# Windowed attention with a split-precision FFN on one core: where the values and scores of the next units stand in TensorE's queue

## The chip, the core and the metric

The kernel runs on one NeuronCore of a Trainium2 chip. The number that counts is the device time of one execution in microseconds. Before the change it is 905.27 us, the median of three runs (904.88 to 905.30). Below, PE is TensorE, PEld its weight loads, DVE is VectorE, ACT is ScalarE, POOL is GpSimd and SP is SyncE, whose queue issues most of the transfers.

## The reference

For 8 batches, 8 heads, 576 positions and head size 64, every position attends to itself and to the 63 positions before it. The result, 4608 tokens of 512 numbers, goes through an FFN with a leaky ReLU of slope 0.01:

```
scores = scale * np.matmul(q, k.transpose(0, 1, 3, 2))
mask = (rel >= 0) & (rel < window)              # window = 64
attn = softmax(np.where(mask, scores, -1e9))
x = np.matmul(attn, v)                          # laid out as 4608 x 512
h = x @ w_in                                    # 512 x 2048
g = np.maximum(0.01 * h, h)
out = g @ w_out                                 # 2048 x 512
```

## The kernel before

**The two halves.** Attention works on units of 64 query positions of one batch, all 8 heads at once; there are 72, and a "visit" handles two. The FFN works on chunks of 512 tokens (nine of them, `c`), which is eight units or four visits of attention. Every chunk runs through 16 column tiles (`f`) of 128 columns of the hidden layer.

**One step of the FFN.** A step is one pair of (c, f). `mm1` (L457) makes the column tile: 12 matmuls of 128x128 weights on 512 tokens, because each operand is the sum of a high and a low part (`x`, `wi`) and three of the four products are taken. The result lands in a PSUM bank named `h`. ACT makes the leaky ReLU `g` from it ("leak", L462) and the rounded high part `gh` (L468), and DVE the low part `gl` (L472). `mm2` (L504) multiplies `gh` and `gl` with `wo`, again 12 matmuls, into four accumulators `acc` that stay open over the 16 steps of a chunk. `mm2` always runs one step behind: a step issues `mm1` of its own tile and then `mm2` of the tile before it. After the sixteenth `mm2` of a chunk, four copies (L530) and four transfers (L531) write the chunk's output.

**One visit of attention.** From the third chunk on (`c` = 2 to 8, 112 steps numbered `n`) a visit is spread over two steps of every four. In the step with `n % 4 == 1`:

- `values_2(u)` (L419): 32 matmuls of 64 columns that multiply the finished probabilities `e` of units u and u+1 with `v`; then SP is told to load the next `v` (L145).
- `scores_2(u+2)` (L234): 64 matmuls of 64x64, the scores of the next two units, into two PSUM banks `s`; then SP is told to load the next `k` and `q` (L141, L137).
- `shield_2(u+2)`: DVE scales and masks both banks into `e` (L380, twice), POOL takes the maximum over the keys (L388, once per half), DVE subtracts the first maximum (L393), ACT takes the first exponential (L394).
- `invert_2(u)`, after `mm2`: two additions and a reciprocal on DVE (L431 to L433) of the sums `n`.

In the step with `n % 4 == 2`: `second_2(u+2)` subtracts and exponentiates the second half (L393, L394), `norm_2(u)` multiplies the values with the reciprocal and writes their high and low part into the `x` of the next chunk (L440, L443, L444), and `sums_2(u+2)` lets POOL add up the exponentials (L406, twice).

**What sets the order.** Every engine works through its own queue strictly in the order in which this code issues instructions; the end of the kernel pins that order with an explicit dependency from each instruction to the one before it on its engine. Semaphores between engines come from the tiles that the instructions share. PSUM banks are handed out in turn: `of_h` alternates between the banks "o" and "h" for `mm1`, and `of_a` between "s" and "t". `scores_2` takes one bank of each kind and `values_2` one of `of_a`. The first two chunks run from other loops (a hand-written order, then a loop over 16 jobs), which already has five visits of its own.

Of the kernel before, what the change touches and what calls it, by code (L numbers as in the profile page):

```python
# [82 lines left out]
def flat(t):  # L83
    return t.rearrange("p a b -> p (a b)") if len(t.shape) == 3 else t
# [3 lines left out]
def band_attention_ffn(ctx: ExitStack, tc: tile.TileContext, qT, kB, vW, w_in, w_out, eye_mask, out):  # L88
# [9 lines left out]
    def bank(tag, name):  # L98
        return ps_e.tile([P, 512], F32, tag=tag, name=name)
# [140 lines left out]
    def mask_of(u):  # L240

        kinds = [v % NQB == 0 for v in (u, u + 1)]
        if any(kinds):
            return away[:, 1:] if kinds[0] else away[:, :2]
        return away[:, :1]
# [115 lines left out]
    def scores_2(u):  # L361
        if u >= NU:
            return
        ps = [bank(next(t), f"s{u}_{j}") for j, t in enumerate((of_a, of_h))]
        quarter_scores(u // 2, ps, False)
        probs[u] = ps
        load_k(u // 2 + 1)
        load_q(u // 2 + 2)

    def shield_2(u):  # L370

        if u >= NU:
            return
        ps = probs.pop(u)
        a = mask_of(u).bitcast(F32)
        n = a.shape[1]
        a = flat(a)[:, None, :].broadcast_to([P, H // n, n * QB])
        for j in range(2):
            e, s = (x.rearrange("a (b c) -> a b c", c=n * QB) for x in (probs_of[:, j], ps[j]))
            nc.vector.scalar_tensor_tensor(e, s, SCALE, a, ALU.mult, ALU.add)  # L380
            if j == 0:
                first_most = most(u, j)
        exps_2(0, first_most)
        probs[u] = most(u, 1)

    def most(u, j):
        mx = wk.tile([P, 512], F32, tag="pT", bufs=1, name=f"mx{u}_{j}")
        nc.gpsimd.partition_all_reduce(mx, probs_of[:, j], P, ReduceOp.max)  # L388
        return mx

    def exps_2(j, mx):
        e = probs_of[:, j]
        nc.vector.tensor_tensor(e, e, mx, ALU.subtract)  # L393
        nc.scalar.activation(e, e, AF.Exp)  # L394

    def second_2(u):

        if u < NU:
            exps_2(1, probs.pop(u))

    def sums_2(u):
        if u >= NU:
            return
        raw = flat(wk.tile([P, 512, 2], U32, tag="raw", bufs=3, name=f"n{u}")).bitcast(F32)
        for j in range(2):
            nc.gpsimd.partition_all_reduce(raw[:, 512 * j : 512 * j + 512], probs_of[:, j], P, ReduceOp.add)  # L406
        probs[u] = raw

    def values_2(u):
        if u >= NU:  # L410
            return
        raw = probs.pop(u)
        v = [v_heads(u // 2, w) for w in range(2)]
        ps = bank(next(of_a), f"o{u}")
        for w in range(2):
            for p in range(NP):
                for j in range(2):
                    c = (2 * p + w) * QB
                    nc.tensor.matmul(  # L419
                        ps[64 * j : 64 * j + 64, c : c + QB], v[w][:, 2 * p + j, :D], probs_of[:, j, c : c + QB],  # L420
                        start=True, stop=True,
                    )
        probs[u, 0] = ps, raw
        load_v(u // 2 + 1)

    def invert_2(u):
        if u >= NU:
            return
        ps, raw = probs[u, 0]
        r, t = raw[:, :512], raw[:, 512:]  # L430
        nc.vector.tensor_scalar_add(r[:64], r[:64], 1e-9)  # L431
        nc.vector.tensor_scalar_add(r[64:], t[64:], 1e-9)
        nc.vector.reciprocal(r, r)  # L433

    def norm_2(u):
        if u >= NU:
            return
        ps, raw = probs.pop((u, 0))
        r, t = raw[:, :512], raw[:, 512:]
        nc.vector.tensor_tensor(t, ps, r, ALU.mult)  # L440
        hi, lo = x_of(u)
        t = t.rearrange("a (b c) -> a b c", b=NP)
        nc.scalar.copy(hi, t)  # L443
        nc.vector.tensor_tensor(lo, t, hi.bitcast(F32), ALU.subtract)  # L444
# [5 lines left out]
    def mm1(c, f, part):  # L450

        xh, xl = xs[c]
        ps = bank(next(of_h) if c or f >= half else "h", f"h{c}_{f}_{part.start}")[:, part]
        wh, wl = wi[f]
        terms = [(a, b, k) for k in range(KT) for a, b in ((wh, xh), (wh, xl), (wl, xh))]
        for n, (a, b, k) in enumerate(terms):
            nc.tensor.matmul(ps, a[:, k, :], b[:, k, part], start=n == 0, stop=n == len(terms) - 1)  # L457
        t = []

        def leak():  # L460
            t.append(wk.tile([P, CH], F32, tag="g", bufs=1, name=f"g{c}_{f}_{part.start}")[:, part])
            nc.scalar.activation(t[0], ps, AF.Prelu, alpha=0.01)  # L462

        def high():
            g[c, f, part.start] = [
                wk.tile([P, CH], F32R, tag=n, name=f"{n}{c}_{f}_{part.start}") for n in ("gh", "gl")
            ]
            nc.scalar.copy(g[c, f, part.start][0][:, part], t[0])  # L468

        def low():  # L470
            hi, lo = (x[:, part] for x in g[c, f, part.start])
            nc.vector.tensor_tensor(lo, t[0], hi.bitcast(F32), ALU.subtract)  # L472

        return leak, high, low
# [13 lines left out]
    def mm2(c, f, part):  # L488


        gh, gl = g.pop((c, f, part.start))
        wh, wl = wo[f]
        for i in range(part.start // P, part.stop // P):
            split = c == 1 or c == 0 and i < 2
            begin = f == 0 or split and f == half
            end = f == FT - 1 or split and f == half - 1
            if begin:
                pool, tag = (ps_o, f"o{i}")
                if c == 1 and f == 0 and i > 1:
                    pool, tag = ps_e, "st"[i - 2]  # L500
                acc[c, i] = pool.tile([P, DM], F32, tag=tag, name=f"acc{c}_{i}_{f}")
            ts = slice(i * P, (i + 1) * P)
            for n, (a, b) in enumerate(((gh, wh), (gh, wl), (gl, wh))):
                nc.tensor.matmul(  # L504
                    acc[c, i], a[:, ts], b, start=begin and n == 0, stop=end and n == 2
                )
            if end:
                due.append(partial(evict, c, i, f, split))
# [24 lines left out]
    def flush():  # L533
        while due:
            due.pop(0)()

    whole, first, second = slice(0, CH), slice(0, CH // 2), slice(CH // 2, CH)
# [33 lines left out]
    def step(name):  # L571
        kind = name.rstrip("0123456789")
        return partial(acts[kind], int(name[len(kind) :]))
# [32 lines left out]
    steps = [(c, f) for c in range(2, NCHUNK) for f in range(FT)]  # L606
    for n, (c, f) in enumerate(steps):
        u = 3 * UPC + n // 4 * 2
        for step in mm1(c, f, whole):
            step()  # L610
        if n % 4 == 1:
            values_2(u)
            scores_2(u + 2)
            shield_2(u + 2)
        if n % 4 == 2:
            second_2(u + 2)
            norm_2(u)
            sums_2(u + 2)
        mm2(*prev)
        flush()  # L620
        if n % 4 == 1:
            invert_2(u)
        prev = (c, f, whole)
# [58 lines left out]
```

## Time and profile before

| | |
|---|---|
| median of the runs | 905.27 us |
| the profiled execution's own time | 906.58 us |
| its span (first to last instruction) | 904.8 us |
| PE busy | 896.4 us (99%) |
| PEld, DVE, POOL, ACT busy | 735.6, 497.2, 321.2, 304.9 us |
| granted TensorE clock | 1.00 |

The profiled execution's time has 1.8 us outside the span and is 1.3 us above the median of the runs. A timeline row gives the start, the duration, the engine, the line of the code, the operation, what it writes and reads, its shape and how many instructions were merged (x12); in brackets stands how long the engine was idle before it and what released it. The ends of matmuls are modelled and overlap the next matmul's start, so PE's pace is read from start to start and not from durations.

### The profile page before, as it was taken

To read this page: it belongs to the slowest core of one execution; us is meant where nothing else is said; L and a number is where in the kernel's file an instruction comes from. 1 tells how busy PE (TensorE), PEld (TensorE's weight loads), DVE (VectorE), ACT (ScalarE), POOL (GpSimd) and SP (SyncE) were. 2 spreads that over 40 slices of the span, in tenths; PEclk is the share of its full clock that TensorE was granted. 3 is DMA by queue.
4 is the path that set the end of the run, shared out by engine and by line. 5 is a ranking of instruction groups with operands and counts; after the bars stand their busy time and mean duration, and the time that the engine had idled before them with its cause. 6 is when DMAs were issued, how large, how long until landed. Compare 5 with 4: busy or idle time off the path is not lost.

```text
span 904.8 us, 16195 instructions
## 1 busy us (share of the span) xinstructions
PE 896.4 (99%) x7021; PEld 735.6 (81%) x7021; DVE 497.2 (55%) x638; ACT 304.9 (34%) x517; POOL 321.2 (36%) x132
## 2 busy tenths in 40 slices
PE   8999999999999999999999999999999999999998
PEld 5887888888888888888888888888888888888886
DVE  6999892388644545555555545444555555531111
ACT  4665654232222232223322222223222332223222
POOL 4422000577433434444444434333434444400000
PEclk9999999999999999999999999999999999999999
DMA  7753741223311011111211121112101221001001
GB/s 286 254 175 116 245 140 70 71 95 119 118 47 47 27 63 53 48 48 47 95 47 49 47 95 47 49 47 85 40 25 40 72 71 36 25 1 47 0 1 47
DMA packets 31895, 68.68 MB, mean 76 GB/s; under 512 B 3024, under 2 KB 3152, under 8 KB 31824
## 3 DMA queue, kind: packets, MB, share of 16 engines
q1 hardware_dynamic: 27360, 51.95, 16.9%
q10 hardware_dynamic: 4464, 15.70, 5.7%
q8 instruction: 55, 0.90, 0.4%
q14 instruction: 16, 0.13, 0.0%
HBM read 56.62 MB, written 11.01 MB: 75 GB/s over the span
## 4 chain that ended last, share of the span: by engine, by line
PE 93%; DVE 4%; issue 1%; DMA 1%; ACT 1%; POOL 0%; ACTq 0%; DVEq 0%
PE acc L504 42%; PE h L457 41%; PE s L234 4%; PE o L419 3%; PE o L323 1%; DMA room<-eye_mask 1%; PE s L268 1%; DVE gl L472 1%; DVE raw L185 1%; DVE w L202 0%; DVE raw L189 0%; DVE raw L197 0%; DVE wi L209 0%; PE s L302 0%; DVE e L293 0%
## 5 line engine op out<-in xcount | busy, mean ns | idle before, releaser
L457 PE MATMUL h<-x,wi 128*128 128x512 f32 (+1 forms) x1440 | 339.1, 384 | 0.1
L457 PEld LDWEIGHTS h<-x,wi 128*128 128x128 f32 x1440 | 265.7, 188 | 54.7 <-DVE x L444 0.4
L504 PE MATMUL acc<-wo,gh 128*128 128x512 f32 x936 | 293.7, 395 | 0.3 <-DVE s L521 0.3
L472 DVE TENSOR_TENSOR gl<-g,gh 128x512 fp32r<-128x512 f32 (+1 forms) x147 | 100.2, 682 | 325.1 <-ACT gh L468 324.9
L388 POOL PARTITION_ALL_REDUCE mx<-e x56 | 108.2, 1933 | 382.1 <-DVE e L380 359.1
L504 PEld LDWEIGHTS acc<-wo,gh 128*128 128x128 f32 x936 | 172.7, 188 | 37.6 <-DVE s L521 0.5
L406 POOL PARTITION_ALL_REDUCE n<-e x56 | 183.2, 3271 | 38.6 <-ACT e L394 38.6
L462 ACT ACTIVATE g<-h 128x512 f32<-128x512 f32 (+1 forms) x147 | 86.6, 589 | 317.0 <-PE h L457 315.8
L504 PE MATMUL acc<-wo,gl 128*128 128x512 f32 x468 | 182.3, 390 | 0.0
L504 PEld LDWEIGHTS acc<-wo,gl 128*128 128x128 f32 x468 | 87.9, 188 | 19.0
L394 ACT ACTIVATE e<-e 128x512 f32<-128x512 f32 x56 | 35.4, 633 | 200.0 <-DVE e L393 200.0
L433 DVE RECIPROCAL n<-n 128x512 f32<-128x512 f32 x28 | 93.9, 3353 | 1.0
L468 ACT CAST gh<-g 128x512 fp32r<-128x512 f32 (+1 forms) x147 | 89.9, 612 | 9.0 <-PE acc L504 4.0
L457 PE MATMUL h<-x,w 128*128 128x512 f32 x324 | 77.8, 389 | 0.0
L444 DVE TENSOR_TENSOR x<-n,x 128x512 fp32r<-128x512 f32 x28 | 61.7, 2202 | 19.2 <-ACT x L443 19.2
L457 PEld LDWEIGHTS h<-x,w 128*128 128x128 f32 x324 | 60.8, 188 | 12.7
L504 PE MATMUL acc<-w,gh 128*128 128x512 f32 x216 | 66.7, 390 | 0.0
L393 DVE TENSOR_TENSOR e<-e,mx 128x512 f32<-128x512 f32 x56 | 38.4, 686 | 36.9 <-POOL mx L388 36.9
L504 PEld LDWEIGHTS acc<-w,gh 128*128 128x128 f32 x216 | 40.5, 188 | 8.5
L234 PE MATMUL s<-q,k 64*64 64x64 f32 x2160 | 41.0, 226 | 1.1 <-DMA q<-qT 1.1
L504 PE MATMUL acc<-w,gl 128*128 128x512 f32 x108 | 42.0, 389 | 0.0
L234 PEld LDWEIGHTS s<-q,k 64*64 64x64 f32 x2160 | 36.3, 140 | 5.7 <-issue 2.1
(70 smaller groups left out, 508.8 us busy)
## 6 DMA issues: line engine op xcount, KB each, us to landing
v<-vW SPq DMA_DIRECT2D x32, 520.0 KB, 4.7
q<-qT SPq DMA_DIRECT2D x34, 256.0 KB, 4.7
k<-kB SPq DMA_DIRECT2D x33, 256.0 KB, 4.6
raw<-w_out ACTq DMA_DIRECT2D x15, 512.0 KB, 3.7
out<-o SPq DMA_DIRECT2D x30, 256.0 KB, 2.2
raw<-w_in ACTq DMA_DIRECT2D x14, 512.0 KB, 3.8
room<-vW SPq DMA_DIRECT2D x4, 520.0 KB, 5.8
sum<-e SPq DMA_DIRECT2D x6, 256.0 KB, 2.0
```

The source lines that it names most:

```text
L234: nc.tensor.matmul(ps[j][t, c : c + QB], k[i][s, p], q[s, w, p], start=not begun and (not more or (w, p) == (0, 0)), stop=not begun and no ...
L388: nc.gpsimd.partition_all_reduce(mx, probs_of[:, j], P, ReduceOp.max)
L393: nc.vector.tensor_tensor(e, e, mx, ALU.subtract)
L394: nc.scalar.activation(e, e, AF.Exp)
L406: nc.gpsimd.partition_all_reduce(raw[:, 512 * j : 512 * j + 512], probs_of[:, j], P, ReduceOp.add)
L433: nc.vector.reciprocal(r, r)
L444: nc.vector.tensor_tensor(lo, t, hi.bitcast(F32), ALU.subtract)
L457: nc.tensor.matmul(ps, a[:, k, :], b[:, k, part], start=n == 0, stop=n == len(terms) - 1)
L462: nc.scalar.activation(t[0], ps, AF.Prelu, alpha=0.01)
L468: nc.scalar.copy(g[c, f, part.start][0][:, part], t[0])
L472: nc.vector.tensor_tensor(lo, t[0], hi.bitcast(F32), ALU.subtract)
L504: nc.tensor.matmul(acc[c, i], a[:, ts], b, start=begin and n == 0, stop=end and n == 2)
```

## The change

In the 112 steps from the third chunk on, the three calls of the visit's first step move from behind `mm1` to ahead of it. Nothing is added or removed.

```diff
     for n, (c, f) in enumerate(steps):
         u = 3 * UPC + n // 4 * 2
-        for step in mm1(c, f, whole):
-            step()
         if n % 4 == 1:
             values_2(u)
             scores_2(u + 2)
             shield_2(u + 2)
+        for step in mm1(c, f, whole):
+            step()
         if n % 4 == 2:
             second_2(u + 2)
             norm_2(u)
             sums_2(u + 2)
         mm2(*prev)
         flush()
         if n % 4 == 1:
             invert_2(u)
         prev = (c, f, whole)
```

`mm1` returns the leak, the rounding and the low part as three functions that are called at once, so these three move with the column tile on ACT and DVE. On PE the place is the beginning of the second visit of chunk 2 (step 5); the first number behind `h`, `g`, `gh` and `gl` is the column tile, the last one counts buffers, and `mx_0` is the maximum of the first half. Before, the tail of the step's own column tile stands ahead of the values:

```order
L457 MATMUL h_5_0_2828<-x_2_2112,wi_0_96 128x512
L457 MATMUL h_5_0_2828<-x_2_2111,wi_1_97 128x512
L419 MATMUL o_2847<-e,v 64x64 [waits DMAHW7_49]
L419 MATMUL o_2847<-e,v 64x64 x15
L234 MATMUL s_0_2865<-q_82,k_85 64x64 [waits DMAHW6_49]
L234 MATMUL s_1_2866<-q_82,k_85 64x64 [waits Activation_49]
```

And now the values follow `mm2` of step 3's tile:

```order
L504 MATMUL acc_3_0_2718<-wo_0_118,gh_3_0_2781 128x512
L504 MATMUL acc_3_0_2718<-wo_1_119,gh_3_0_2781 128x512
L504 MATMUL acc_3_0_2718<-wo_0_118,gl_3_0_2782 128x512
L419 MATMUL o_2828<-e,v 64x64 [waits DMAHW7_49]
L419 MATMUL o_2828<-e,v 64x64 x15
L234 MATMUL s_0_2846<-q_82,k_85 64x64 [waits DMAHW6_49]
```

The column tile `h_5` now stands behind the scores, where it is followed by `mm2` of step 4's tile; a wait for ACT in front of the scores' second bank is gone. On DVE, in the same visit, before:

```order
L472 TENSOR_TENSOR gl_5_0_2844<-g_5_0_2841,gh_5_0_2843 128x512
L380 SCALAR_TENSOR_TENSOR e<-s_0_2865,away 128x512
L380 SCALAR_TENSOR_TENSOR e<-s_1_2866,away 128x512
L393 TENSOR_TENSOR e<-e,mx_0_2902 128x512
L431 TENSOR_SCALAR n_2751<-n_2751 64x512
L432 TENSOR_SCALAR n_2751<-n_2751 64x512
L433 RECIPROCAL n_2751<-n_2751 128x512
L472 TENSOR_TENSOR gl_6_0_2940<-g_6_0_2937,gh_6_0_2939 128x512
```

And now:

```order
L380 SCALAR_TENSOR_TENSOR e<-s_0_2846,away 128x512
L380 SCALAR_TENSOR_TENSOR e<-s_1_2847,away 128x512
L393 TENSOR_TENSOR e<-e,mx_0_2883 128x512
L472 TENSOR_TENSOR gl_5_0_2906<-g_5_0_2903,gh_5_0_2905 128x512
L431 TENSOR_SCALAR n_2751<-n_2751 64x512
L432 TENSOR_SCALAR n_2751<-n_2751 64x512
L433 RECIPROCAL n_2751<-n_2751 128x512
L472 TENSOR_TENSOR gl_6_0_2940<-g_6_0_2937,gh_6_0_2939 128x512
```

The low part `gl_5` has moved from ahead of the masking to between the first subtraction and the additions. ACT mirrors it; here is the whole of the difference in this visit, the exponential (L394) moving ahead of the leak and the rounding of tile 5:

```order
-L462 ACTIVATE g_5_0_2841<-h_5_0_2828 128x512
-L468 CAST gh_5_0_2843<-g_5_0_2841 128x512
-L394 ACTIVATE e<-e 128x512
+L394 ACTIVATE e<-e 128x512
+L462 ACTIVATE g_5_0_2903<-h_5_0_2890 128x512
+L468 CAST gh_5_0_2905<-g_5_0_2903 128x512
```

The orders of SP and POOL are the same as before.

## The prediction

> **What bounds the kernel now.** I read the page's head and chain of waits first, then the busy times by stretch, and then one visit on the timeline.
>
> ```profile
> PE 896.4 (99%) x7021; PEld 735.6 (81%) x7021; DVE 497.2 (55%) x638; ACT 304.9 (34%) x517; POOL 321.2 (36%) x132
> PE 93%; DVE 4%; issue 1%; DMA 1%; ACT 1%; POOL 0%; ACTq 0%; DVEq 0%
> 303.97:328.17 24.20, 24.20 (x194) 19.98 (x193) 12.82 (x13) 6.73 (x11) 10.32 (x4) 1.00 0.13 44
> 328.17:352.37 24.20, 24.20 (x194) 19.98 (x193) 11.78 (x12) 8.68 (x15) 9.54 (x4) 1.00 0.27 89
> 230.00:810.00 580.00, 580.00 (x4546) 478.43 (x4545) 306.28 (x314) 170.26 (x283) 239.29 (x93) 1.00 0.16 53
> ```
>
> PE sets the end, and in the stretch that the change touches (230 to 810 us) its 580.00 us are busy without a gap, at the full granted clock. Four steps with one visit take 24.20 us, on an ordinary visit (first window) as on one behind a chunk's end (second). Since a busy PE is a modelled quantity, the pace has to be read from starts. PE alone, one visit:
>
> ```profile
> 403.49 0.61 PE L504 MATMUL acc<-wo,gh 128*128 128x512 f32 x2
> 406.21 2.88 PE L457 MATMUL h<-x,w 128*128 128x512 f32 x12
> 409.02 1.15 PE L419 MATMUL o<-e,v 128*64 128x64 f32 x32
> 410.10 1.16 PE L234 MATMUL s<-q,k 64*64 64x64 f32 x64
> 411.19 0.74 PE L504 MATMUL acc<-wo,gh 128*128 128x512 f32 x2
> 414.09 2.88 PE L457 MATMUL h<-x,w 128*128 128x512 f32 x12
> 416.81 0.61 PE L504 MATMUL acc<-w,gh 128*128 128x512 f32 x2
> ```
>
> An undisturbed block of 12 big matmuls takes 2.72 us (403.49 to 406.21, and 414.09 to 416.81). The block ahead of the values takes 2.81 (406.21 to 409.02): entering the small matmuls costs 0.09. The values take 1.08, the scores 1.09, and the block behind the scores 2.90 (411.19 to 414.09): leaving them costs 0.18. So 8 x 2.72 + 0.09 + 1.08 + 1.09 + 0.18 = 24.20: every tenth of the period is accounted for, and none of it is a wait. Only 0.27 us per visit is not matmul work, and with 24 visits (the last without scores) the ceiling of any gain is 24 x 0.27 = 6.5 us.
>
> **The change on PE: the same blocks, other neighbours.** It adds and removes no instruction. Entering now comes behind `mm2` instead of `mm1`; leaving comes into `mm1` instead of `mm2`. Both pairs occur in the hand-written part:
>
> ```profile
> 82.04 0.39 PE L504 MATMUL acc<-wo,gl 128*128 128x512 f32 x1
> 82.36 0.69 PE L323 MATMUL o<-room,e 128*64 128x65 f32 x16
> 71.57 3.02 PE L457 MATMUL h<-x,wi 128*128 128x512 f32 x12
> 74.52 0.69 PE L323 MATMUL o<-v,e 128*64 128x65 f32 x16
> 163.64 0.73 PE L504 MATMUL acc<-wo,gh 128*128 128x512 f32 x2
> 166.50 0.84 PE L457 MATMUL h<-x,w 128*128 128x512 f32 x3
> ```
>
> Behind `mm2`, the next start comes 0.32 us after the last big one (82.04 to 82.36) against an ordinary 2.72 / 12 = 0.23: 0.09, as behind `mm1`. At 71.57 an `mm1` follows scores and takes 2.95 to the next start; that includes an entry into small matmuls (0.09), so leaving cost 0.14. An `mm2` behind scores that had no values ahead of them (163.64 to 166.50) took 2.86, again 0.14. So the partner does not matter in these rows, and the steady 0.18 has 0.04 more because values and scores follow each other, which they still do. I take 0 for both. Bounds: leaving lies between the cheapest row below, 0.12 (190.65 to 193.49, a block of 2.84), and 0.18 plus another 0.04, so 23 x (-0.06 to +0.04) = -1.4 to +0.9 us; the two entry rows agree to 0.01, so 24 x 0.01 = 0.2 either way.
>
> ```profile
> 190.65 0.73 PE L504 MATMUL acc<-wo,gh 128*128 128x512 f32 x2 [0.34 <-DVE s L521]
> 193.49 0.84 PE L457 MATMUL h<-x,wi 128*128 128x512 f32 x3
> ```
>
> The Trainium skill bears on the 0.27. Its page "TensorEngine Tiling (Array Packing)", section Key Properties, says that changing the tiling mode drains TensorE. The shapes in the rows (128*128, 128*64, 64*64) change three times per visit before and after the change, so by that rule the sum is 0 if every drain costs the same, and 905.3 us stays; if a drain is longer behind `mm2` than behind `mm1`, it speaks against this change, and the third rival below is that case.
>
> **The change on DVE, ACT and POOL.** What could open a gap in PE is a result that comes late. The same visit, the other engines:
>
> ```profile
> 403.69 0.60 ACT L462 ACTIVATE g<-h 128x512 f32<-128x512 f32 x1 [4.13 <-PE h L457]
> 409.75 0.62 ACT L468 CAST gh<-g 128x512 fp32r<-128x512 f32 x1
> 410.40 0.69 DVE L472 TENSOR_TENSOR gl<-g,gh 128x512 fp32r<-128x512 f32 x1 [4.75 <-ACT gh L468]
> 411.38 1.29 DVE L380 SCALAR_TENSOR_TENSOR e<-s,away 128x512 f32<-128x512 f32 x2 [0.29 <-PE s L234]
> 412.17 1.78 POOL L388 PARTITION_ALL_REDUCE mx<-e  x1 [11.66 <-DVE e L380]
> 413.98 0.69 DVE L393 TENSOR_TENSOR e<-e,mx 128x512 f32<-128x512 f32 x1 [1.31 <-POOL mx L388]
> 414.77 0.63 ACT L394 ACTIVATE e<-e 128x512 f32<-128x512 f32 x1 [4.40 <-DVE e L393]
> 414.59 0.41 DVE L431 TENSOR_SCALAR n<-n 64x512 f32<-64x512 f32 x1
> 416.22 3.35 DVE L433 RECIPROCAL n<-n 128x512 f32<-128x512 f32 x1
> 420.75 0.63 ACT L394 ACTIVATE e<-e 128x512 f32<-128x512 f32 x1 [2.43 <-DVE e L393]
> 421.47 3.23 POOL L406 PARTITION_ALL_REDUCE n<-e  x1 [1.40 <-ACT e L394]
> 422.00 2.26 DVE L444 TENSOR_TENSOR x<-n,x 128x512 fp32r<-128x512 f32 x1 [0.69 <-ACT x L443]
> 424.97 1.29 PE L457 MATMUL h<-x,wi 128*128 128x512 f32 x5
> ```
>
> I re-time it with these durations. The values start at 406.21 + 0.09 = 406.30, the scores end at 408.47 (before: 411.19), so everything that hangs on the scores comes 2.72 earlier: masking 408.66 to 409.95, first maximum from 409.45, first subtraction 411.26 to 411.95, first exponential 412.05 to 412.68. The column tile runs 408.47 to 411.37, and its leak could start 0.20 later (403.49 to 403.69), at 411.57, but it stands behind the exponential: 412.68 to 413.28. Then the rounding to 413.91 and `gl` from about 413.94 to 414.63. Four things wait there:
>
> - `mm2` of this tile comes after `mm2` of the last one and another `mm1`, at 408.47 + 2.90 + 2 x 2.72 = 416.81, as now. `gh` is ready 2.9 us, `gl` (wanted two matmuls later, 417.26) 2.6 us before that.
> - The next `mm1` (414.09) takes the bank of a score half, which is free at 409.95.
> - The additions of `invert_2` now stand behind `gl`: neighbours on DVE overlap by 0.08 (413.98 + 0.69 is 414.67, and the additions start at 414.59), so they would start at 414.55; today it is 414.59. The chain reciprocal, next `gl`, second subtraction, normalization, `x` therefore stays where it is to within 0.1. It is the tightest one: at a chunk's end `x` is done at 422.00 + 2.26 = 424.26, and the next chunk's `mm1` starts at 424.97, 0.71 us of cover.
> - The values themselves need the second exponential (done 421.38) and the masking needs POOL's sums over `e` to be done (421.47 + 3.23 = 424.70); the next visit's values would start at 430.50 and its masking at 432.86: 9.1 and 8.2 us of cover.
>
> Behind a chunk's end, four output copies stand on ACT ahead of the visit:
>
> ```profile
> 430.41 2.88 PE L457 MATMUL h<-x,wi 128*128 128x512 f32 x12
> 434.31 0.59 ACT L530 COPY o<-acc 128x512 f32<-128x512 f32 x1 [1.73 <-DMA out<-o]
> 434.79 0.60 ACT L462 ACTIVATE g<-h 128x512 f32<-128x512 f32 x1
> 441.01 0.61 PE L504 MATMUL acc<-wo,gh 128*128 128x512 f32 x2
> ```
>
> There the first subtraction would end at 430.41 + 5.74 = 436.15 (411.95 lies 5.74 behind 406.21) and the exponential at 436.9, after the copies (434.90), so they hold up nothing; `gh` is done at 438.1, 2.9 us before 441.01. Transfers: SP's order is unchanged, its loads of `v`, `k` and `q` are released up to 2.72 us earlier and land in some 5 us of a 24.20 us period:
>
> ```profile
> v<-vW SPq DMA_DIRECT2D x32, 520.0 KB, 4.7
> q<-qT SPq DMA_DIRECT2D x34, 256.0 KB, 4.7
> ```
>
> **The sum.** 0 on PE, 0 on what PE waits for: the profiled execution's 906.58 us (904.8 of span) stays. The median of the runs, 905.27, is 1.3 lower and stays with it: **905.3 us**.
>
> **The rivals.**
> - *Leaving gets cheaper, faster.* If the column tile behind the scores hid the whole leaving cost, 23 x 0.18 = 4.1 us would go: 901.1. For it: the loads of `mm1`'s weights wait for nothing that the visit makes. Against: 0.14 at 71.57, the same pair. To count, 0.08 of the 0.18 has to go. 7%.
> - *The `x` chain slips, slower.* `gl` now has to pass the exponential, the leak and the rounding before the additions may start. If it came later than computed by more than the cover (0.71 + 0.04), each chunk start from 3 to 7 would stall (chunk 8's last visit has no scores), five in all. If the first maximum took the 3.23 that POOL's sums take and not 1.78, the slip is 1.45 and the price 5 x (1.45 - 0.75) = 3.5: 908.8. Against: the rows above repeat alike. It decides from 0.75 + 1.81 / 5 = 1.1 us of slip on. 5%.
> - *Entering gets dearer, slower.* If the values had to wait for one more whole big matmul (0.23) behind `mm2`, 24 x 0.23 = 5.5 us: 910.8; it decides from 0.08 a visit on. For it: entering costs 0.09 already. Against: 82.04 to 82.36, the same pair without it. 3%. By the Trainium skill's "TensorEngine Tiling (Array Packing)", Key Properties, that wait would be the drain; row 82.36 does not show a longer one.
> - *Hardly a change.* That it does not do what it says is ruled out by the order; its effect can still be nothing, which is the forecast: 85%.
>
> **How the numbers follow.** A difference under 0.2% (1.8 us) cannot be told from none here. The forecast's own bounds are -1.6 to +1.1 us; no case outside it holds more than 7%, so the range is these bounds, rounded up on the slow side for a small part of the `x` chain: 903.7 to 906.6. Faster by over 0.2%: 7%; within: 85%; slower: 8%.
>
> **What would show it.** Right: PE busy without a gap between 230 and 810 us and 24.20 us for each visit, `h` behind the scores in about 2.90 us, the first exponential directly ahead of the leak on ACT, `gl` ending about 2.6 us before its use, `x` done about 0.7 us before a chunk's first `mm1`. Wrong: a block behind the scores under 2.82 or over 2.98 us, or an idle time ahead of `mm1` put down to `x` (L444) at a chunk's start.

## The result, and the profile after

The changed kernel takes 910.27 us (median; 910.12 to 910.54) against 905.28 us before (904.88 to 906.42): 1.0052 of the time before, with an interval from 1.0040 to 1.0064. It is slower by 5.0 us where no change was forecast. The page of the changed kernel, whose profiled execution took 910.12 us:

```profile
span 908.3 us, 16167 instructions
PE 894.7 (99%) x7021; PEld 732.6 (81%) x7021; DVE 537.5 (59%) x638; ACT 300.9 (33%) x517; POOL 314.5 (35%) x132
PE 82%; DVE 10%; issue 3%; ACT 2%; POOL 1%; DMA 1%; ACTq 0%; DVEq 0%
```

DVE does the same 638 instructions and is busy 40.3 us longer (537.5 against 497.2), and the chain of waits, which ran over PE for 93% of the span, now leaves it for DVE, ACT and POOL. PE's busy time has not grown, so what is lost is waiting. Two stretches of four steps, an ordinary one and one that begins with chunk 3, and all waits of PE from 230 us on:

```profile
303.05:327.25 24.20, 24.20 (x194) 19.98 (x192) 14.52 (x14) 6.52 (x11) 10.02 (x5) 1.00 0.14 44
327.25:352.28 25.03, 24.50 (x194) 19.90 (x192) 14.52 (x14) 8.67 (x15) 10.01 (x5) 1.00 0.25 86
```

```profile
PE h L457 <- DVE x L444: 2.7, 5, 0.5
```

The ordinary stretch still takes 24.20 us, to the hundredth. The one that starts a chunk takes 0.83 more, and five times `mm1` waits for the low part of `x` (the row shows the idle share of it, 2.7 us; from start to start, each of the five blocks takes 3.55 instead of 2.72). 5 x 0.83 = 4.2 us. In the two profiled spans (904.8 and 908.3) there is besides 0.9 us less ahead of chunk 2 and 0.3 us more behind the last matmul: 4.2 - 0.9 + 0.3 = 3.5, their difference. Of the 5.0 us between the medians, 4.2 are thus located and the rest lies inside the interval (3.6 to 5.8 us).

Why `x` is late shows in one visit, the last one of chunk 3, on all engines:

```profile
406.21 1.15 PE L419 MATMUL o<-e,v 128*64 128x64 f32 x32
407.29 1.16 PE L234 MATMUL s<-q,k 64*64 64x64 f32 x64
408.38 3.06 PE L457 MATMUL h<-x,w 128*128 128x512 f32 x12
411.28 0.62 PE L504 MATMUL acc<-wo,gh 128*128 128x512 f32 x2
411.96 1.78 POOL L388 PARTITION_ALL_REDUCE mx<-e  x1 [0.82 <-DVE e L393]
412.24 0.63 ACT L394 ACTIVATE e<-e 128x512 f32<-128x512 f32 x1 [7.39 <-DVE e L393]
412.77 0.58 ACT L462 ACTIVATE g<-h 128x512 f32<-128x512 f32 x1
413.39 0.62 ACT L468 CAST gh<-g 128x512 fp32r<-128x512 f32 x1
413.65 3.31 POOL L406 PARTITION_ALL_REDUCE n<-e  x1
414.04 2.47 DVE L472 TENSOR_TENSOR gl<-g,gh 128x512 fp32r<-128x512 f32 x1 [2.17 <-ACT gh L468]
416.44 0.80 DVE L431 TENSOR_SCALAR n<-n 64x512 f32<-64x512 f32 x1
417.25 0.42 DVE L432 TENSOR_SCALAR n<-n 64x512 f32<-64x512 f32 x1
417.70 3.35 DVE L433 RECIPROCAL n<-n 128x512 f32<-128x512 f32 x1
423.48 2.26 DVE L444 TENSOR_TENSOR x<-n,x 128x512 fp32r<-128x512 f32 x1 [0.69 <-ACT x L443]
425.80 2.79 PE L457 MATMUL h<-x,wi 128*128 128x512 f32 x11 [0.53 <-DVE x L444]
```

`gl` starts at 414.04, where it was expected, and then takes 2.47 us instead of 0.69. POOL's first sum has started 0.39 us ahead of it. (In the 22 other visits with scores the sum is 0.12 us ahead and `gl` takes 2.75 us, so that it ends at the same place.) The sum needs the first exponential, which is done at 412.87; it starts right behind POOL's second maximum, which now ends at 413.74. Everything behind `gl` on DVE moves: the reciprocal starts at 417.70 instead of 416.22, and `x` is done at 425.74 instead of 424.26. The next chunk's `mm1` starts at 424.88, but its second matmul, the first one that reads the low part of `x`, waits until 425.80.

### The profile page after: what moved, and what is told of

Its sections match the earlier page's. It is cut to its first block, busy times and chain, and to the rows that moved or that the text cites. A ratio compares the mean times of both kernels' runs of the same rounds, so it can differ in the third digit from the quotient of the medians.

```text
span 908.3 us, 16167 instructions
## 1 busy us (share of the span) xinstructions
PE 894.7 (99%) x7021; PEld 732.6 (81%) x7021; DVE 537.5 (59%) x638; ACT 300.9 (33%) x517; POOL 314.5 (35%) x132
## 4 chain that ended last, share of the span: by engine, by line
PE 82%; DVE 10%; issue 3%; ACT 2%; POOL 1%; DMA 1%; ACTq 0%; DVEq 0%
PE h L457 37%; PE acc L504 37%; PE s L234 4%; PE o L419 3%; DVE gl L472 2%; DVE x L444 1%; POOL mx L388 1%; DVE e L393 1%; DVE raw L185 1%; DVE raw L197 1%; DVE raw L189 1%; DVE w L202 1%; DMA room<-eye_mask 1%; PE o L323 1%; DVE e L380 0%
## 5 line engine op out<-in xcount | busy, mean ns | idle before, releaser
L457 PE MATMUL h<-x,wi 128*128 128x512 f32 (+1 forms) x1440 | 343.7, 387 | 2.7 <-DVE x L444 2.7
L504 PE MATMUL acc<-wo,gh 128*128 128x512 f32 x936 | 289.8, 391 | 0.3 <-DVE s L521 0.3
L472 DVE TENSOR_TENSOR gl<-g,gh 128x512 fp32r<-128x512 f32 (+1 forms) x147 | 147.3, 1002 | 229.1 <-ACT gh L468 228.9
L504 PEld LDWEIGHTS acc<-wo,gh 128*128 128x128 f32 x936 | 174.6, 188 | 37.0 <-DVE s L521 0.5
L388 POOL PARTITION_ALL_REDUCE mx<-e x56 | 101.1, 1805 | 289.1 <-DVE e L380 266.2
L394 ACT ACTIVATE e<-e 128x512 f32<-128x512 f32 x56 | 35.4, 632 | 275.1 <-DVE e L393 275.1
L433 DVE RECIPROCAL n<-n 128x512 f32<-128x512 f32 x28 | 93.9, 3353 | 1.0
L380 DVE SCALAR_TENSOR_TENSOR e<-s,away 128x512 f32<-128x512 f32 x56 | 36.0, 684 | 66.9 <-PE s L234 66.9
L444 DVE TENSOR_TENSOR x<-n,x 128x512 fp32r<-128x512 f32 x28 | 61.7, 2203 | 19.2 <-ACT x L443 19.2
```

The lines of the kernel that those rows point to most:

```text
L504: nc.tensor.matmul(acc[c, i], a[:, ts], b, start=begin and n == 0, stop=end and n == 2)
```

## The experiments

My theory after this comparison (A): `gl` is slow because POOL's first sum now runs beside it, and the additions, the reciprocal and `x` stand behind `gl`; the time is lost only where a chunk's start waits for that `x`. Its rivals: `gl` is late by its place alone, behind the exponential, the leak and the rounding (B); or a little is lost on PE at every visit (C).

### One part of the change alone, and the other

e3 moves only the last visit of each chunk ahead of the column tile, e4 all the others:

```diff
+        first = n % 16 == 13        # e4: != 13
-        if n % 4 == 1:
+        if n % 4 == 1 and first:
             values_2(u)
             scores_2(u + 2)
             shield_2(u + 2)
         for step in mm1(c, f, whole):
             step()
+        if n % 4 == 1 and not first:
+            values_2(u)
+            scores_2(u + 2)
+            shield_2(u + 2)
```

> Only the last visit of each chunk (step 13 of 16; six of the 24 visits) comes ahead of the column tile; the other eighteen stay behind it as before. Theory A: only a visit that a chunk's start waits for costs time, so all five stalls of 0.83 us stay: 909.5 to 910.3 us. Rival C (a little at every visit): 6 of 24 of 5.0 us, 906.5 us.

> The opposite: all visits but the last of each chunk come ahead of the column tile (eighteen of 24). Theory A: gl is as slow as in the changed kernel at the moved visits, about 2.4 us, but no stall at the chunk starts: 905.3 us (ratio 0.999 to 1.001). Rival C: 18 of 24 of 5.0 us, 909.0 us.

e3 took 910.18 us against 905.69 (ratio 1.0052, 1.0040 to 1.0065): six of 24 visits carry the whole loss. e4 took 905.85 (1.0004, 0.9995 to 1.0012): eighteen visits carry none. C falls. The waits of PE in e3, its longest:

```profile
PE h L457 <- DVE x L444: 2.7, 5, 0.5
```

These are the same five waits of the same size as in the changed kernel; e4 has no wait on PE in this stretch. DVE and POOL in e4, a moved visit and the next one, which is the last of its chunk and was left behind the column tile:

```profile
388.11 3.31 POOL L406 PARTITION_ALL_REDUCE n<-e  x1
388.22 2.75 DVE L472 TENSOR_TENSOR gl<-g,gh 128x512 fp32r<-128x512 f32 x1 [1.90 <-ACT gh L468]
397.95 2.26 DVE L444 TENSOR_TENSOR x<-n,x 128x512 fp32r<-128x512 f32 x1 [0.69 <-ACT x L443]
408.97 0.69 DVE L472 TENSOR_TENSOR gl<-g,gh 128x512 fp32r<-128x512 f32 x1 [4.74 <-ACT gh L468]
420.57 2.26 DVE L444 TENSOR_TENSOR x<-n,x 128x512 fp32r<-128x512 f32 x1 [0.69 <-ACT x L443]
```

In the moved visit `gl` is slow and `x` late, and nobody minds; the one visit whose `x` PE waits for has the fast `gl`.

### POOL's two sums in the other order

Neither sum can start ahead of the second exponential when the second half's sum comes first, so POOL is idle while `gl` runs. PE, ACT and DVE keep the changed order.

```diff
     def sums_2(u):
-        for j in range(2):
+        for j in (1, 0):
             nc.gpsimd.partition_all_reduce(raw[...], probs_of[:, j], P, ReduceOp.add)
```

> The changed kernel, with one edit: POOL adds up the second half of the exponentials ahead of the first half, so that neither sum can start before the second exponential, and POOL is idle while gl of the visit's column tile runs. Theory A (gl is slow because POOL's first sum now runs beside it, and the additions, reciprocal and x wait behind gl): gl there falls from 2.47 us to about 0.69, x is done about 1 us ahead of the next chunk's first column tile, the five stalls of 0.83 us at the starts of chunks 3 to 7 are gone, and the time is that of the kernel before, 905.3 us (ratio to it 0.999 to 1.001). Rival B (gl is late by its place alone, behind the exponential, the leak and the rounding, whatever POOL does): the stalls stay and the time is about 910. Rival C (the time is lost a little at every visit, on TensorE itself): about 910.

It took 916.24 us (ratio 1.0116, 1.0101 to 1.0132), a miss for A and no proof of B: `sums_2` also serves the visits of the first two chunks, which come every two steps and have no time for late sums. PE there, from the timeline of e1:

```profile
206.02 1.16 PE L419 MATMUL o<-e,v 128*64 128x64 f32 x32 [1.89 <-ACT e L394]
222.63 1.98 PE L419 MATMUL o<-e,v 128*64 128x64 f32 x32 [3.25 <-ACT e L394]
242.15 2.79 PE L457 MATMUL h<-x,wi 128*128 128x512 f32 x11 [1.36 <-DVE x L444]
```

PE waits up to 3.25 us for late exponentials there, and `mm1` of chunk 2 starts at 240.4 us instead of 230.2. From 266 us on e1 has no stall at a chunk's start. So e6 swaps the sums only from the third chunk on, and e7 does the same to the kernel before (`sums_2` takes the order of the halves as an argument; the lines that add it are left out here):

```diff
-            sums_2(u + 2)
+            sums_2(u + 2, (1, 0))       # in the loop over chunks 2 to 8 only
```

> The changed kernel with POOL's two sums swapped as in e1, but only from the third chunk on. The trace of e1 lost its time before 266 us, in the visits of the first two chunks, which come every two steps; from there on it had no stall. Theory A (POOL's first sum beside gl, and the x chain behind gl): with the swap kept out of the first chunks the time is that of the kernel before, 905.3 to 905.8 us (ratio 0.999 to 1.001), gl of the visit's tile takes 0.69 us and x is done about 1.6 us ahead of the next chunk's first column tile. Rival B (gl late by its place alone): 910. Rival D (the swap itself costs time at every visit, as the 916 of e1 could also be read): above 912.

> The control: the kernel before (visit behind the column tile) with the same swap of POOL's two sums from the third chunk on. In the old order gl runs ahead of the masking and never met the first sum, and the x chain had 0.71 us of cover. Theory A: no change in time, 905.3 to 905.8 us (ratio 0.999 to 1.001). Rival D: above 912.

e6 took 905.12 us against 905.16 (0.9999, 0.9990 to 1.0008): the loss is gone, with the changed order of PE. A visit of e6 on POOL, DVE and PE:

```profile
412.74 0.69 DVE L472 TENSOR_TENSOR gl<-g,gh 128x512 fp32r<-128x512 f32 x1 [2.18 <-ACT gh L468]
413.34 0.41 DVE L431 TENSOR_SCALAR n<-n 64x512 f32<-64x512 f32 x1
413.77 0.42 DVE L432 TENSOR_SCALAR n<-n 64x512 f32<-64x512 f32 x1
419.48 6.70 POOL L406 PARTITION_ALL_REDUCE n<-e  x2 [7.05 <-ACT e L394]
420.01 2.26 DVE L444 TENSOR_TENSOR x<-n,x 128x512 fp32r<-128x512 f32 x1 [0.69 <-ACT x L443]
423.56 2.88 PE L457 MATMUL h<-x,wi 128*128 128x512 f32 x12
```

With POOL idle, `gl` takes 0.69 us in the very same place, and `x` is done at 422.27, 1.29 us ahead of the chunk's first `mm1` (in the other visits the sums and `x` come 0.27 us earlier). B falls. The collision is not gone but has moved: in the 22 other visits the `gl` of the tile two steps later starts 0.05 us behind the second of the two sums and takes 2.82 us, at no cost in the time; no chain to `x` stands behind it. The control e7 took 906.16 (1.0010, 1.0001 to 1.0019), not the 912 of the rival D, but above the 905.3 to 905.8 that A gave it; its steps from chunk 3 on take what they took before, and 0.9 us of the 1.0 appears in its profile behind the last matmul. Why there was not looked into.

### The collision left, the chain unhooked

e5 keeps `gl` beside POOL's sum and issues the additions and the reciprocal one step earlier, where DVE has room (a line of `invert_2` that looks up the sums changes with it and is left out):

```diff
         u = 3 * UPC + n // 4 * 2
+        if n % 4 == 0:
+            invert_2(u)
         if n % 4 == 1:
             values_2(u)
...
-        if n % 4 == 1:
-            invert_2(u)
```

> The changed kernel, with the two additions and the reciprocal of the sums issued one step earlier, at the beginning of the step with n % 4 == 0, where DVE has room: gl no longer stands ahead of them. The collision of gl with POOL stays. Theory A: gl of the visit's tile still takes about 2.4 us, but x no longer waits for it and is done 1 to 3 us ahead of the next chunk; no stalls: 905.3 us (ratio 0.999 to 1.001). Rival B gives the same here, since the chain is unhooked from gl. Rival C: about 910.

905.78 us against 905.69 (1.0002, 0.9993 to 1.0010). The rows of DVE and POOL in e5:

```profile
413.14 3.31 POOL L406 PARTITION_ALL_REDUCE n<-e  x1
413.54 2.47 DVE L472 TENSOR_TENSOR gl<-g,gh 128x512 fp32r<-128x512 f32 x1 [2.17 <-ACT gh L468]
420.27 2.26 DVE L444 TENSOR_TENSOR x<-n,x 128x512 fp32r<-128x512 f32 x1 [0.69 <-ACT x L443]
```

`gl` is as slow as in the changed kernel, and `x` is done at 422.53, 1.84 us ahead of the chunk's `mm1` at 424.37. Both halves of A are thus needed for the loss: the slow `gl`, which e6 removed, and the chain behind it, which e5 removed.

### What of `gl` collides

In e8 the leak writes back into its PSUM bank, so `gl` has only one operand in SBUF:

```diff
         def leak():
-            t.append(wk.tile([P, CH], F32, tag="g", ...)[:, part])
+            t.append(ps if c > 1 else wk.tile([P, CH], F32, tag="g", ...)[:, part])
             nc.scalar.activation(t[0], ps, AF.Prelu, alpha=0.01)
```

> The changed kernel, with one edit from the third chunk on: the leak writes its result back into its PSUM bank instead of a tile in SBUF, so that gl reads one operand from PSUM and only one from SBUF. POOL's first sum still starts ahead of gl and runs beside it. Theory A1 (what blocks gl is that both of its operands come from SBUF while POOL reads SBUF): gl takes about 0.7 us beside the sum, the additions follow at once, x is done before the next chunk's column tile, no stalls: 905.2 to 905.9 us. Theory A2 (any DVE write to SBUF, or any DVE instruction, is slowed beside that sum): gl stays at about 2.5 us, the five stalls of 0.83 us stay: about 910 us.

907.32 us against 905.13 (1.0025, 1.0015 to 1.0035), between the two forecasts. DVE and POOL in e8, and PE's weight loads waiting:

```profile
412.38 3.31 POOL L406 PARTITION_ALL_REDUCE n<-e  x1
412.46 0.69 DVE L472 TENSOR_TENSOR gl<-h,gh 128x512 fp32r<-128x512 f32 x1 [1.86 <-ACT gh L468]
413.07 1.91 DVE L431 TENSOR_SCALAR n<-n 64x512 f32<-64x512 f32 x1
414.99 0.98 DVE L432 TENSOR_SCALAR n<-n 64x512 f32<-64x512 f32 x1
416.00 3.35 DVE L433 RECIPROCAL n<-n 128x512 f32<-128x512 f32 x1
```

```profile
PEld h L457 <- DVE x L444: 2.6, 5, 0.5
```

A1 is right on `gl`: inside the sum it takes 0.69 us. What neither theory had: the additions that follow now meet the same sum and take 1.91 and 0.98 instead of 0.41 and 0.42. Five stalls remain, of 0.39 to 0.43 us from start to start; 5 x 0.41 = 2.1 us, against 2.2 measured. None of these kernels beats the one before: with four of PE's steps at 24.20 us as before there is nothing to win here but the stalls that the change brought.

## Why the prediction was wrong

- **The change on PE: right.** The ordinary stretch takes 24.20 us as before. The column tile behind the scores takes 2.90 us (408.38 to 411.28), as forecast from the scores into `mm2`; e4, e5 and e6 keep this order at no cost. Entering the values behind `mm2` costs 0.09 us as forecast (a block of 2.81 us at all 24 visits). The ceiling on a gain was not put to the test, since no kernel gained.
- **The additions behind `gl`: the step that failed.** The prediction re-timed the visit "with these durations", and gave `gl` 0.69 us, "about 413.94 to 414.63". Its start was right within 0.2 us (7.83 us behind the start of the values, 7.55 in the other visits, 7.64 forecast); its duration was 2.47, and 2.75 in the others. So the chain over the additions to `x` did not stay "where it is to within 0.1". I moved the masking, the first maximum, the first subtraction and the first exponential by 2.72 us, but not what POOL does next, the second maximum and the first sum. In the kernel before, these two came long after `gl` (410.40):

```profile
414.77 2.09 POOL L388 PARTITION_ALL_REDUCE mx<-e  x1 [0.82 <-DVE e L393]
415.02 1.17 DVE L432 TENSOR_SCALAR n<-n 64x512 f32<-64x512 f32 x1
416.77 3.31 POOL L406 PARTITION_ALL_REDUCE n<-e  x1
```

The sum stands at 413.65 now, 3.12 us earlier: 2.72 with the scores, 0.31 because the maximum ahead of it takes 1.78 us instead of 2.09, and 0.09 because PE is that much ahead of the old clock. The second addition won 0.75 us back, because it no longer meets a maximum (1.17 before, 0.42 now), and the first lost 0.39. In all `x` slips by 1.57 us against PE. The prediction's cover of 0.71 was too small, since only the second matmul of a chunk reads the low part of `x`, 0.23 us later: 0.94. Of the 1.57, 0.63 are left; with 0.06 from the end of `x` to the matmul it starts 0.69 late (425.80 instead of 425.11), and the 11 matmuls from there on take 0.14 more than usual (2.63 us). That makes the 0.83 at each chunk's start.
- **The price was in the profile before.** The prediction quoted the row of `x` without asking why it was so long. In the kernel before, by group from 230 to 800 us, and the spread of `x`:

```profile
L444 DVE TENSOR_TENSOR x<-n,x 128x512 fp32r<-128x512 f32 x24 | 54.2, 2258 | 16.5 <-ACT x L443 16.5
L432 DVE TENSOR_SCALAR n<-n 64x512 f32<-64x512 f32 x24 | 27.4, 1140 | 0.4
L431 DVE TENSOR_SCALAR n<-n 64x512 f32<-64x512 f32 x24 | 9.9, 411 | 0.0
L433 DVE RECIPROCAL n<-n 128x512 f32<-128x512 f32 x24 | 80.5, 3353 | 0.8
```

```profile
L444 DVE TENSOR_TENSOR x<-n,x x28: 692/2258/2260, 187.7 to 806.3; 128x512 fp32r<-128x512 f32 x28
```

`x` (L444) has the shape of `gl` and takes 2258 ns beside a sum; in the last visit, where POOL has nothing left to do, it takes 692. L432 does what L431 does on as many numbers and takes 1140 instead of 411 ns, beside a maximum. A `gl` that meets a sum had its price in these rows. They also say why the cover of `x` was so small: before and after, `x` itself is held up beside the visit's second sum.
- **The rival "the `x` chain slips": right in place, close in price, wrong in its cause, and too unlikely.** It named the five chunk starts and 5 x (slip - 0.75); with the measured slip of 1.57 that is 4.1 us, against 4.2 located. That these agree is in part luck: the cover was 0.94, and the 0.2 us that each late block loses besides make up for it. It looked for the slip in a longer maximum and got 5% because "the rows above repeat alike", which holds only while nothing on POOL moves.
- **The other covers.** `gl` was to be 2.6 us ahead of its use; it is done at 416.51, some 0.66 us ahead of 417.17. That one nearly became a stall at 23 visits. The copies at a chunk's end and the bank of the scores held up nothing, as forecast.

## What to carry to other kernels

When an instruction moves earlier, everything it releases on every engine moves too; write down for each of them what it now runs beside, not only what waits for it. A row whose mean is far above that of a like operation on the same engine is a price tag: find out what it ran beside before using the shorter one elsewhere. On an engine that works in order, a chain with little cover should not stand behind an operation whose duration depends on a neighbour; e5 took it out of there at no cost.

## What the runs showed of the hardware

DVE and POOL hold each other up over some operands, and the shape of it was sharper than I had thought. `gl` ends 2.86 us after the sum's start whether it started 0.11 us behind it (e4: 388.11, 390.97) or 0.39 us (after: 413.65, 416.51), so it is held until a point and not slowed by a share. Its last 0.69 us are its own work, so that point lies some 2.17 us behind the sum's start. With one operand in PSUM it is not held at all (e8: 0.69 us). A subtraction of two SBUF tiles and an addition of a constant to one are held. In e8 the first addition gets through at the same point (413.07 + 1.91 - 0.41 = 414.57, 2.19 us behind the sum's start), and the second is then held again until 3.17 us behind it (414.99 + 0.98 - 0.42 = 415.55).

It goes the other way too: POOL waits when DVE came first. The second maximum takes 2.09 us in the kernel before, where an addition started 0.18 us ahead of it, and 1.78 us in the changed one, where none did. In the visit of e6 above, a `gl` (422.39) started 0.23 us ahead of the second sum and took 0.69 us, and the two sums took 6.70 us; in the 22 other visits that sum came first, `gl` took 2.82 us and the two sums 6.45.

The reciprocal, from one SBUF tile to itself, takes 3353 ns on average over 24 in the kernel before, where it starts 0.55 us ahead of the sum in all but the last visit, and the same in the changed kernel, where it starts after it. The sum takes 3.31 us in both, so a reciprocal ahead of it does not hold it up; none started inside a sum, so whether a sum would hold up a reciprocal is not shown.

The Trainium skill states this on its page "SBUF — State Buffer", section Who interferes with whom: a DVE instruction with two SBUF inputs contends with a GpSimd instruction that reads SBUF, one in a 2-port mode contends with GpSimd as well, and whichever is issued second is blocked entirely. The traces agree that the second one is held and that it is not shared; in which mode the additions run, no trace shows. They show `gl` let go at about 415.82 (416.51 - 0.69), 1.14 us ahead of the sum's recorded end (413.65 + 3.31 = 416.96), POOL's spans being rough. An estimate by that rule and the recorded end has `gl` end at 416.96 + 0.69 = 417.65, behind its use at 417.17; the measured end is 416.51, and no such stall appeared.
